# A spectral filter and a gated feed-forward layer on one core: every step in a new order, and some sums and low parts on GpSimd

## The chip, the core and the metric

The kernel runs on one core of a Trainium2 chip. The number that counts is the device time of one execution in microseconds, the median of several runs. The kernel before takes 406.75 us (runs of 407.12, 405.2 and 406.75). TensorE (PE) does the matmuls, VectorE (DVE), ScalarE (ACT) and GpSimd (POOL) the elementwise work. The hardware queue of transfers is issued by SyncE (SP); POOL issues a queue of its own.

## The reference

```python
xn = (x - mean(x)) / sqrt(var(x) + 1e-5)          # x: 2048 x 512
X = rfft2(xn) * (w_r + 1j * w_i)                   # over both axes; 2048 x 257 bins
s = irfft2(X)                                      # 2048 x 512
gate = xn @ W_gate; up = xn @ W_up                 # 512 -> 1376 each
h = where(gate > 0, gate, 0) * up
g = silu(h @ W_down)                               # 1376 -> 512
out = x + s * g
```

## The kernel before

Both halves are matmuls. A number is held as a high and a low f16 part, and each product is made in three passes (high by high, high by low, low by high).

**Feed-forward half.** The 2048 rows are four blocks of 512, the 1376 hidden columns eleven groups of 128 (the last, number 10, has 96). `gu` is a PSUM tile of a gate or an up product (12 matmuls of 512 columns); there are three buffers of it. ACT makes `r` = relu(gate), DVE `h32` = gate times up, ACT its high part `h16`, DVE the low part, and `dn` is the product with W_down, 512 columns by 128 rows of output at a time, one PSUM buffer. ACT turns it into the gate `g`.

For some pairs of hidden groups in the last block, `fast_products` (L1049) makes the four products of a pair from fewer matmuls with sums of rows (`xS`) and of weights (`wT`, made by `weight_sums`, L788, from the weights in `rp`): three PSUM tiles `sa`, `sb`, `sc` take products of 256 columns in turn, ACT copies `sb`<-`sa`, `sk`<-`sc`, DVE adds `sc`, `se`<-`sb`+`sk`, ACT relus to `sr` and `sq`, and DVE multiplies. PE cannot make the next product into `sb` or `sc` before these are through. In the rows of the order below, `se3_4` is the `se` of block 3, pair 4, and `sv4_4640` the `sv` of chunk 4 (the last number is the instance); the trace leaves the numbers out.

**Spectral half.** Two-dimensional transforms as matmuls with constant matrices: `s` (rows), `y`, `xx` (columns), then the filter on DVE and POOL (`tt` products, their sums `pf`, rounded to `p`), and back by `z`, `v` and a second `s`. There are eight chunks. `fold` (L651) prepares the sums and differences of a chunk's input. `last_stage` (L1293) of chunk c takes the second `s` from PSUM with ACT (`zz`), makes sums and differences (`ae`, `ye`, `sv`), and `finish` (L1342) multiplies `sv` by `g`. The second `s` needs a PSUM buffer of the same ring as `gu`.

**Output.** For chunks 0, 1, 3 and 4 (`ADDS`, L45) the copy of x goes to `out` first and `sv` is then added by a DMA on POOL's queue, `out<-sv`, two per chunk. For the others DVE adds x in the tile `xt`, which SP stores. `sv`, `ye`, `eo`, `x` and more share a ring of ten buffers, `k4` (`ROOM`, L56): whoever takes a buffer waits until the last reader of its former holder is done, and where this is a DMA, until it has landed. `columns` (L172) parts the last 128 rows of output into 256, 128 and 128 columns (`dn_3`, `dn_3b`, `dn_3bb`), so that the last gate, multiply, add and store are smaller.

**Order.** All work is stated as steps of one engine with a cost, what they read and write, and a due time. `Plan.run` (L244) places them one by one: on each engine, of the steps that can begin soonest, that with the earliest due time. Due times and the lead with which some steps may begin come from two tables of numbers (`DUES`, `WAITS`). The order that results is the order of the instructions on each engine, which then waits in line: an instruction that waits holds up all behind it. Every instruction goes through the one helper at L189, so all rows of the trace name that line (in the changed kernel, which has one line more, L190).

Lists of engine names say where some work is done: `FOLDS`, `SUM2` (the sums `tt` and `pf`), `DIFF2` (`ae`), `TSUMS` (sums of weights of a pair), `SECONDS` and `HLOWS` (the second multiply, `se`, and the low parts in `fast_products`). In `fast_products` the multiply is `lambda: eng.tensor_mul(T[E], T[E], T[r2])` (L1095): it looks up `eng` when it is run, and by then the loop behind it has set `eng` anew, to the engine of the pair's second low part. Its cost and its place in the plan are those of `SECONDS`.

Of the kernel before, what the change touches and what calls it, by code (L numbers as in the profile page):

```python
# [54 lines left out]
SUM2, DIFF2 = ['POOL', 'POOL', 'DVE', 'POOL', 'DVE', 'DVE', 'POOL', 'DVE', 'POOL', 'DVE', 'DVE', 'POOL', 'POOL', 'DVE', 'DVE', 'POOL'], ['DVE', 'POOL', 'POOL', 'POOL', 'POOL', 'DVE', 'DVE', 'DVE', 'POOL', 'DVE', 'POOL', 'DVE', 'POOL', 'DVE', 'DVE', 'POOL']  # L55
ROOM = {"k4": 10, "k2": 8, "kg": 4, "cm": 3, "h16": 11, "xg": 3, "F": 2, "gu": 3, "dn": 1, "q": 4, "q4": 2, "mv": 4, "m": 4, "p": 4, "am": 1, "mid": 3}  # L56
CALM, SAFE, SAFE_LAG, RATE, TURNKB = 40, 1.0, 1.0, 320, 1300
SUMS, TSUMS, FMARGIN = ['DVE', 'DVE', 'DVE', 'DVE'], ['DVE', 'DVE', 'DVE', 'DVE', 'DVE'], 0.4
SECONDS, HLOWS = ['DVE', 'DVE', 'DVE', 'DVE', 'DVE', 'DVE', 'DVE', 'DVE', 'DVE', 'DVE', 'DVE', 'DVE', 'DVE', 'DVE', 'DVE', 'DVE', 'DVE', 'DVE', 'DVE', 'DVE'], ['DVE', 'DVE', 'DVE', 'DVE', 'DVE', 'DVE', 'DVE', 'DVE', 'DVE', 'DVE', 'DVE', 'DVE', 'DVE', 'DVE', 'DVE', 'DVE', 'DVE', 'DVE', 'DVE', 'DVE', 'DVE', 'DVE', 'DVE', 'DVE', 'DVE', 'DVE', 'DVE', 'DVE', 'DVE', 'DVE', 'DVE', 'DVE', 'DVE', 'DVE', 'DVE', 'DVE', 'DVE', 'DVE', 'DVE', 'DVE']
# [311 lines left out]
def kernel(ctx: ExitStack, tc: tile.TileContext, x, wg, wu, wd, wl, ew, sp, c_r, c_d, c_m, c_x, c_s, out):  # L371
    nc = tc.nc
    PS = bass.MemoryType.PSUM
    PE, DVE, ACT, POOL, SP = (InOrder(tc, e) for e in (nc.tensor, nc.vector, nc.scalar, nc.gpsimd, nc.sync))
# [47 lines left out]
    step = T.step  # L422
# [1139 lines left out]
```

## Time and profile before

| | |
|---|---|
| median of three runs | 406.75 us (405.2 to 407.12) |
| profiled execution | 405.83 us |
| its span, first to last instruction | 404.1 us |
| busy PE / DVE / ACT / POOL | 395.1 / 327.0 / 234.7 / 30.3 us |
| granted clock of PE | 1.00 |

The profiled execution's 405.83 us is 1.7 us more than the span that the trace covers, and 0.9 us less than the median of the runs. A busy PE is not a PE at its peak, since matmuls overlap; but an idle PE is plain. Idle time of the other engines costs only where somebody waits for it, and a wait in a queue is charged to the instruction that waits, though those behind it pay too.

### The profile page before, as it was taken

The page shows a single profiled execution, that of the slowest core. Times are in us where ns is not written, and L with a number is a line of the kernel's source. Part 1 is how long each engine was busy: PE and PEld are TensorE (multiplying, and loading weights), DVE is VectorE, ACT ScalarE, POOL GpSimd, SP SyncE. Part 2 cuts the span into 40 slices and gives each one's busy share as a digit, 9 for nine tenths or more (in the row PEclk, how much of TensorE's full clock was granted, in tenths as well). Part 3 has the DMA queues.
Part 4 walks back from the last instruction along what each step waited for, and adds up shares of the span by engine and source line. Part 5 has one row for each costly group of instructions (what it writes and reads, how often), then busy time and mean ns, then how long its engine had stood idle before and what let it go on. Part 6 is the DMA issues. An engine that isn't in the chain of part 4 may idle for free.

```text
span 404.1 us, 8177 instructions
## 1 busy us (share of the span) xinstructions
PE 395.1 (98%) x3152; PEld 225.6 (56%) x3152; DVE 327.0 (81%) x733; ACT 234.7 (58%) x458; POOL 30.3 (8%) x48
## 2 busy tenths in 40 slices
PE   8999999999999999999999999999999999989995
PEld 7864444444444454565564545646557767766455
DVE  4899999998889899457749699889973838779985
ACT  6899986788668785141345454746335636634321
POOL 0000000000000000003101001020110003303300
PEclk9999999999999999999999999999999999999999
DMA  7955004824996668831053445368391499649654
GB/s 262 407 223 174 0 2 110 182 57 138 300 309 183 170 220 289 280 82 52 26 170 84 141 128 173 86 200 212 79 233 55 131 217 253 121 120 195 166 191 149
DMA packets 52791, 66.37 MB, mean 164 GB/s; under 512 B 20432, under 2 KB 30256, under 8 KB 52752
## 3 DMA queue, kind: packets, MB, share of 16 engines
q1 hardware_dynamic: 51600, 63.76, 53.4%
q0 software_dynamic: 1152, 2.10, 3.5%
q8 instruction: 24, 0.39, 0.4%
q14 instruction: 15, 0.12, 0.1%
HBM read 42.76 MB, written 20.99 MB: 158 GB/s over the span
## 4 chain that ended last, share of the span: by engine, by line
PE 89%; DMA 4%; ACT 4%; DVE 1%; issue 0%; SPq 0%; POOL 0%; DVEq 0%; ACTq 0%
PE gu L189 42%; PE dn L189 27%; PE sb L189 3%; PE s L189 3%; PE z L189 3%; PE xx L189 3%; ACT wgu L189 2%; PE sa L189 2%; PE sc L189 2%; DMA out<-sv 2%; PE y L189 2%; PE v L189 2%; DMA raw<-in_wu 2%; DVE sv L189 1%; DMA x<-in_x 1%; PE dn_3bb L189 0%
## 5 line engine op out<-in xcount | busy, mean ns | idle before, releaser
L189 PE MATMUL gu<-xT,wgu 128*128 128x512 f16 (+1 forms) x768 | 167.2, 372 | 0.9 <-ACT r L189 0.6
L189 PEld LDWEIGHTS <-wgu 128*128 128x128 f16 x960 | 92.7, 98 | 87.4 <-issue 3.7
L189 PE MATMUL dn<-wds,h 128*128 128x512 f16 (+2 forms) x528 | 116.9, 372 | 0.0
L189 PEld LDWEIGHTS <-h 128*128 128x128 f16 (+1 forms) x594 | 54.4, 98 | 56.5 <-issue 2.2
L189 DVE TENSOR_TENSOR h<-gu,r 128x512 f32<-128x512 f32 (+3 forms) x44 | 27.6, 627 | 10.0 <-PE gu L189 8.9
L189 ACT ACTIVATE r<-gu 128x512 f32<-128x512 f32 (+2 forms) x36 | 20.9, 579 | 25.1 <-PE gu L189 25.0
L189 ACT ACTIVATE h<-h 128x512 f16<-128x512 f32 (+1 forms) x36 | 22.4, 625 | 21.0 <-DVE h L189 20.7
L189 DVE TENSOR_TENSOR h<-h,h 128x512 f16<-128x512 f32 (+1 forms) x36 | 25.1, 700 | 2.5 <-ACT h L189 2.1
L189 POOL TENSOR_TENSOR tt<-tt,tt 128x256 f32<-128x256 f32 x8 | 7.7, 963 | 246.2 <-DVE tt L189 226.9
L189 DVE SCALAR_TENSOR_TENSOR tt<-xsp,cw,wt 128x512 f32<-128x512 f32 x32 | 22.9, 761 | 0.2
L189 ACT ACTIVATE g<-dn,cdi 128x512 f32<-128x512 f32 (+1 forms) x16 | 10.6, 670 | 19.4 <-PE dn L189 15.6
L189 ACT ACTIVATE p<-pf 128x1024 f16<-128x1024 f32 x8 | 8.5, 1057 | 16.5 <-DVE pf L189 15.2
L189 PE MATMUL gu<-xT,wgt 128*64 128x256 f16 (+1 forms) x144 | 17.0, 309 | 0.0
L189 DVE TENSOR_TENSOR z<-z,z 128x1024 f16<-128x1024 f32 x8 | 9.8, 1223 | 8.4 <-ACT z L189 8.3
L189 PEld LDWEIGHTS <-wT 128*128 128x128 f16 x144 | 13.8, 98 | 4.5 <-issue 1.9
L189 DVE SCALAR_TENSOR_TENSOR wgu<-raw,p,wgu 128x512 f16<-128x512 f32 x20 | 14.2, 743 | 0.0
L189 DVE TENSOR_TENSOR xsp<-xx,xo 128x256 f32<-128x256 f32 (+1 forms) x16 | 5.0, 352 | 10.9 <-ACT xsp L189 9.1
L189 PEld LDWEIGHTS <-wgt 128*64 128x64 f16 (+1 forms) x144 | 9.6, 106 | 7.1 <-issue 1.5
L189 ACT ACTIVATE wgu<-raw 128x512 f16<-128x512 f32 x20 | 12.4, 621 | 1.4 <-DMA raw<-in_wu 0.7
L189 PE MATMUL sb<-xS,wT 128*128 128x256 f16 x96 | 11.8, 273 | 1.3 <-DVE sv L189 1.3
L189 POOL TENSOR_TENSOR ae<-zz 128x128 f32<-128x128 f32 (+1 forms) x16 | 8.8, 599 | 53.6 <-ACT zz L189 41.8
L189 DVE TENSOR_TENSOR t<-s,t 128x128 f16<-128x128 f32 (+1 forms) x16 | 10.5, 685 | 2.3 <-ACT t L189 2.3
(197 smaller groups left out, 604.8 us busy)
## 6 DMA issues: line engine op xcount, KB each, us to landing
A_d<-t SPq DMA_DIRECT2D x16, 256.0 KB, 3.5
rw<-in_wl SPq DMA_DIRECT2D x8, 512.0 KB, 5.0
wt<-in_wl SPq DMA_DIRECT2D x8, 512.0 KB, 4.6
at<-A_d SPq DMA_DIRECT2D x8, 512.0 KB, 4.9
C_d<-t SPq DMA_DIRECT2D x16, 256.0 KB, 3.5
ct<-C_d SPq DMA_DIRECT2D x16, 256.0 KB, 7.5
x<-in_x SPq DMA_DIRECT2D x7, 512.0 KB, 4.1
G_d<-g SPq DMA_DIRECT2D x12, 256.0 KB, 2.3
```

The source lines that it names most:

```text
L189: return lambda *args, **kw: self.tc.keep_in_program_order(f(*args, **kw))
```

## The change

Nothing that is computed changes: PE has the same 3152 matmuls. What changes are the numbers of the planner, and the engines named in the lists:

```diff
-FOLDS, FOLD_LEAD, MARGIN = ['DVE', 'DVE', 'DVE', 'DVE', 'DVE', 'DVE', 'DVE', 'DVE'], 78.705, 1.95
+FOLDS, FOLD_LEAD, MARGIN = ['DVE', 'DVE', 'DVE', 'DVE', 'DVE', 'POOL', 'DVE', 'DVE'], 78.705, 1.95
-NORMS = ['DVE', 'DVE', 'DVE', 'DVE', 'DVE', 'ACT', 'ACT', 'DVE', 'DVE', 'DVE', 'ACT', 'DVE', 'DVE', 'ACT', 'DVE', 'DVE']
+NORMS = ['DVE', 'DVE', 'DVE', 'DVE', 'ACT', 'DVE', 'ACT', 'ACT', 'DVE', 'ACT', 'DVE', 'DVE', 'DVE', 'DVE', 'DVE', 'DVE']
-SUM2, DIFF2 = ['POOL', 'POOL', 'DVE', 'POOL', 'DVE', 'DVE', 'POOL', 'DVE', 'POOL', 'DVE', 'DVE', 'POOL', 'POOL', 'DVE', 'DVE', 'POOL'], ['DVE', 'POOL', 'POOL', 'POOL', 'POOL', 'DVE', 'DVE', 'DVE', 'POOL', 'DVE', 'POOL', 'DVE', 'POOL', 'DVE', 'DVE', 'POOL']
+SUM2, DIFF2 = ['POOL', 'POOL', 'POOL', 'POOL', 'POOL', 'POOL', 'POOL', 'POOL', 'POOL', 'POOL', 'POOL', 'POOL', 'DVE', 'DVE', 'POOL', 'DVE'], ['POOL', 'POOL', 'DVE', 'DVE', 'DVE', 'DVE', 'POOL', 'DVE', 'DVE', 'DVE', 'DVE', 'DVE', 'DVE', 'DVE', 'DVE', 'DVE']
-SUMS, TSUMS, FMARGIN = ['DVE', 'DVE', 'DVE', 'DVE'], ['DVE', 'DVE', 'DVE', 'DVE', 'DVE'], 0.4
+SUMS, TSUMS, FMARGIN = ['DVE', 'DVE', 'DVE', 'DVE'], ['POOL', 'DVE', 'POOL', 'DVE', 'POOL'], 0.4
-SECONDS, HLOWS = ['DVE', 'DVE', 'DVE', 'DVE', 'DVE', 'DVE', 'DVE', 'DVE', 'DVE', 'DVE', 'DVE', 'DVE', 'DVE', 'DVE', 'DVE', 'DVE', 'DVE', 'DVE', 'DVE', 'DVE'], ['DVE', 'DVE', 'DVE', 'DVE', 'DVE', 'DVE', 'DVE', 'DVE', 'DVE', 'DVE', 'DVE', 'DVE', 'DVE', 'DVE', 'DVE', 'DVE', 'DVE', 'DVE', 'DVE', 'DVE', 'DVE', 'DVE', 'DVE', 'DVE', 'DVE', 'DVE', 'DVE', 'DVE', 'DVE', 'DVE', 'DVE', 'DVE', 'DVE', 'DVE', 'DVE', 'DVE', 'DVE', 'DVE', 'DVE', 'DVE']
+SECONDS, HLOWS = ['DVE', 'DVE', 'DVE', 'DVE', 'DVE', 'DVE', 'DVE', 'DVE', 'DVE', 'DVE', 'DVE', 'DVE', 'DVE', 'DVE', 'DVE', 'DVE', 'DVE', 'DVE', 'DVE', 'DVE'], ['DVE', 'DVE', 'DVE', 'DVE', 'DVE', 'DVE', 'DVE', 'DVE', 'DVE', 'DVE', 'DVE', 'DVE', 'DVE', 'DVE', 'DVE', 'DVE', 'DVE', 'DVE', 'DVE', 'DVE', 'DVE', 'DVE', 'DVE', 'DVE', 'DVE', 'DVE', 'DVE', 'DVE', 'DVE', 'DVE', 'DVE', 'POOL', 'DVE', 'DVE', 'DVE', 'POOL', 'POOL', 'POOL', 'DVE', 'DVE']
+DEVIATE = (2.68, 2.54, 2.54)
 DUES = (
-    9.45, 123.13, 114.11, 124.55, 1e+09, 1e+09, 1e+09, 1e+09, 1e+09, 1e+09, 1e+09, 1e+09, 1e+09, 1e+09, 1e+09, 1e+09, 1e+09, 1e+09, 1e+09, 1e+09,
...
+    22.97, 129.83, 142.84, 147.2, 1e+09, 1e+09, 1e+09, 1e+09, 1e+09, 1e+09, 1e+09, 1e+09, 1e+09, 1e+09, 1e+09, 1e+09, 1e+09, 1e+09, 1e+09, 1e+09,
...
 WAITS = (
-    7.16, 8.31, 9.25, 95.27, 18.97, 77.25, 61.2, 65.23, 46.59, 33.23, 54.73, 90.53, 33.33, 3.56, 7.82, 116.65, 68.38, 18.19, 7.93, 12.13, 24.01,
...
+    12.95, 9.5, 13.45, 77.89, 13.68, 27.76, 43.2, 22.88, 66.81, 18.05, 88.78, 26.95, 66.35, 2.7, 3, 127.06, 47.09, 50.7, 25.11, 41.31, 30.03, 18.56,
...
-        step("DVE", 2.4 + .14 * sum("ACT" in NORMS[2 * c:2 * c + 2] for c in cs), run, reads=[(f"mv{c}", i) for c in cs for i in range(2 + (STATS[c] == "ACT"))], writes=[(name, 2)], port=True)
+        step("DVE", DEVIATE[cs[0] // 2 - 1], run, reads=[(f"mv{c}", i) for c in cs for i in range(2 + (STATS[c] == "ACT"))], writes=[(name, 2)], port=True)
```

All numbers of `DUES` and `WAITS` are new; a line of each is shown. POOL has 13 entries of `SUM2` where it had 8, and 3 of `DIFF2` where it had 8 (an entry is two instructions). `DEVIATE` is a cost that the planner reckons with and changes no instruction. The entries 31, 35, 36 and 37 of `HLOWS` are low parts in the last block: pair 0's and pair 2's second, and both of pair 3. By the late look-up of `eng` the second multiplies `se` of these three pairs go to POOL too, while the plan has them on DVE.

The first place is SP's queue at the start: the loads of x (`x`), of the gate and up weights (`raw_0`, `raw_1`) and of the constant matrix `cR`. Before:

```order
L189 DMA x_141<-in_x 128x512 x2
L189 DMA raw_1_148<-in_wu 128x512
L189 DMA raw_0_153<-in_wg 128x512
L189 DMA cR<-in_c_r 128x512
L189 DMA x_169<-in_x 128x1024
L189 DMA raw_0_173<-in_wg 128x512
L189 DMA raw_1_186<-in_wu 128x512
```

and now:

```order
L190 DMA x_141<-in_x 128x512 x2
L190 DMA raw_0_148<-in_wg 128x512
L190 DMA raw_1_153<-in_wu 128x512
L190 DMA x_168<-in_x 128x1024
L190 DMA raw_0_172<-in_wg 128x512
L190 DMA raw_1_185<-in_wu 128x512
L190 DMA raw_0_194<-in_wg 128x512
```

with `cR` further behind in the same queue:

```order
L190 DMA raw_1_238<-in_wu 128x1024
L190 DMA raw_1_251<-in_wu 128x896
L190 DMA x_254<-in_x 128x1024
L190 DMA wds<-in_wd 128x3x512
L190 DMA cR<-in_c_r 128x512
```

The load of `cR`, 128 KB, has gone from ahead of the second chunk of x to behind the first load of W_down.

The second place is ACT's queue in the last stages, where a new `sv` takes the buffer in which chunk 1's `sv` was (the wait for two DMASW semaphores is that for its two `out<-sv`). Before, chunk 4's `sv` (`sv4_4640`) takes it:

```order
L189 ACTIVATE h16_3_3_1_4637<-se3_3_4611 128x512 [waits DVE_49]
L189 ACTIVATE sv4_4640<-ye4_4460 128x4 [waits DMASW1_49,DMASW0_49]
L189 ACTIVATE r3_3_4657<-gu3_3_0_4617 128x512 [waits DMAHW3_49,PE_49]
L189 ACTIVATE sv0_4665<-ye0_4559 128x4 [waits DVE_49,Activation_49,Pool_49]
L189 ACTIVATE sv3_4681<-ye3_4593 128x4 [waits DVE_49,Activation_49]
L189 ACTIVATE h16_3_3_0_4688<-sr3_3_4566 128x512 [waits DVE_49]
L189 ACTIVATE sb3_4_4704<-sa3_4_4667 128x512 [waits PE_49]
```

and now chunk 3's (`sv3_4700`), with other work behind it:

```order
L190 ACTIVATE sv4_4697<-ye4_4446 128x4 [waits DVE_49,Activation_49]
L190 ACTIVATE sv3_4700<-ye3_4614 128x4 [waits DMASW1_49,DMASW0_49]
L190 ACTIVATE ye2_4621<-ae2_4568 128x2 [waits DVE_49]
L190 ACTIVATE h16_3_3_0_4710<-sr3_3_4387 128x512
L190 ACTIVATE zz7_4726<-s2_7_4640,cwi_111 128x1024 [waits DVE_49,PE_49,Activation_49]
L190 ACTIVATE zz6_4746<-s2_6_4669,cwi_111 128x1024 [waits DMAHW6_49,DMAHW3_49,PE_49]
L190 ACTIVATE ye7_4751<-zz7_4726 128x2 [waits DMAHW7_49,DMAHW0_49,Activation_49]
L190 ACTIVATE sr3_4_4767<-sa3_4_4599 128x512 [waits PE_49,Pool_49]
```

The wait stands as before, but the relu `r3_3` and the copy of `sa3_4` to `sb3_4` are no longer behind it; the high part of `sr3_3`, the `zz` of chunks 7 and 6 and the relu `sr3_4`, which also waits for POOL, are. DVE has the same wait at its own part of `sv3_4700`.

The third place is POOL's queue in those stages, before:

```order
L189 DMA out_0<-sv1_4414 128x512 x2
L189 TENSOR_TENSOR ae0_4554<-zz0_4534 128x2x63
L189 DMA out_0<-sv4_4640 128x512
L189 DMA out_0<-sv0_4665 128x512 x2
L189 DMA out_0<-sv3_4681 128x512 x2
L189 TENSOR_TENSOR ae5_4914<-zz5_4896 128x2x64
L189 DMA out_0<-sv4_4640 128x512
```

and now:

```order
L190 DMA out_0<-sv1_4415 128x512
L190 TENSOR_TENSOR ae3_4547<-zz3_4524 128x2x64 x2
L190 DMA out_0<-sv1_4415 128x512
L190 TENSOR_TENSOR h16_3_3_0_4710<-sr3_3_4387,h16_3_3_0_4710 128x512
L190 DMA out_0<-sv0_4577 128x512 x2
L190 DMA out_0<-sv4_4697 128x512
L190 DMA out_0<-sv3_4700 128x512
L190 TENSOR_TENSOR se3_3_4543<-se3_3_4543,sq3_3_4572 128x512
L190 DMA out_0<-sv3_4700 128x512
L190 TENSOR_TENSOR h16_3_3_1_4832<-se3_3_4543,h16_3_3_1_4832 128x512
L190 DMA out_0<-sv4_4697 128x512
```

The multiply `se3_3` and two low parts of pair 3 now stand among the additions to `out`.

The last place is the end of SP's queue, before:

```order
L189 DMA out<-xt_1_5103 128x512
L189 DMA out<-xt_1_5121 128x512
L189 DMA out<-xt_1_5074 128x128 x2
L189 DMA out<-xt_0_5129 128x512
L189 DMA out<-xt_1_5074 128x256
```

and now:

```order
L190 DMA out<-xt_0_5066 128x512
L190 DMA out<-xt_0_5060 128x512
L190 DMA out<-xt_0_5090 128x512
L190 DMA out<-xt_1_5068 128x256
L190 DMA out<-xt_1_5068 128x128 x2
```

The part of 256 columns of the last 128 rows of output has gone from last to third last; PE's last matmuls are now of `dn_3b`, 128 columns, in place of `dn_3`, 256.

More of the change, by code (lines that the diff above doesn't have):

```diff
@@ L64 @@
 XDUE, SDUE = [-18.3, 7.83, 88.22, 100.36, 188.84, 115.24, 195.7, 156.37], [-84.52, 3.8, 95.3, 188.33]
+DEVIATE = (2.68, 2.54, 2.54)
 DUES = (
-    9.45, 123.13, 114.11, 124.55, 1e+09, 1e+09, 1e+09, 1e+09, 1e+09, 1e+09, 1e+09, 1e+09, 1e+09, 1e+09, 1e+09, 1e+09, 1e+09, 1e+09, 1e+09, 1e+09,
+    22.97, 129.83, 142.84, 147.2, 1e+09, 1e+09, 1e+09, 1e+09, 1e+09, 1e+09, 1e+09, 1e+09, 1e+09, 1e+09, 1e+09, 1e+09, 1e+09, 1e+09, 1e+09, 1e+09,
     1e+09, 1e+09, 1e+09, 1e+09, 1e+09, 1e+09, 1e+09, 1e+09, 1e+09, 1e+09, 1e+09, 1e+09, 1e+09, 1e+09, 1e+09, 1e+09, 1e+09, 1e+09, 1e+09, 1e+09, 1e+09,
-    1e+09, 1e+09, 1e+09, 1e+09, 1e+09, -211.71, -49.3, -65, -49.5, -49.61, -49.7, -48.72, -47.53, -40.01, -55.32, -41.85, -48.21, -52.55, -46.66,
[83 rows of a table removed]
+    1e+09, 1e+09, 1e+09, 1e+09, 1e+09, -128.45, -85.36, -83.53, -85.74, -105.37, -88.74, -74.4, -87.39, -83.45, -82.92, -84.78, -81.82, -80.12,
[83 rows of a table added]
 )
 WAITS = (
[12 rows of a table removed]
[12 rows of a table added]
 )
```

188 rows, old and new, of tables (DUES, WAITS) are left out of this document.

## The prediction

> **What bounds the kernel now.** First the page: who is busy, where POOL works, and who ends the chain of waits.
>
> ```profile
> PE 395.1 (98%) x3152; PEld 225.6 (56%) x3152; DVE 327.0 (81%) x733; ACT 234.7 (58%) x458; POOL 30.3 (8%) x48
> ...
> POOL 0000000000000000003101001020110003303300
> ...
> PE 89%; DMA 4%; ACT 4%; DVE 1%; issue 0%; SPq 0%; POOL 0%; DVEq 0%; ACTq 0%
> ```
>
> PE is busy in 98% of the span and has 89% of the chain. DVE, the second, has 327.0 us and 1% of the chain: taking work from DVE is worth only what PE waits for DVE. So the question is where PE is idle. The view of busy time by stretch of 10 us has PE at 10.00 everywhere but in these seven rows:
>
> ```profile
> 0.00:10.00 10.00, 8.80 (x62) 7.13 (x63) 4.63 (x19) 6.49 (x16) 1.00 (x8) 1.00 0.77 260
> 10.00:20.00 10.00, 9.30 (x77) 8.20 (x76) 8.41 (x27) 8.96 (x25) 0.00 (x0) 1.00 1.03 408
> 20.00:30.00 10.00, 9.44 (x71) 6.65 (x69) 9.14 (x32) 9.61 (x28) 0.00 (x0) 1.00 0.62 233
> 90.00:100.00 10.00, 9.66 (x65) 4.38 (x64) 8.85 (x28) 8.74 (x18) 0.00 (x0) 1.00 0.43 130
> 350.00:360.00 10.00, 8.13 (x62) 5.82 (x60) 7.39 (x20) 4.07 (x10) 0.00 (x0) 1.00 0.58 148
> 390.00:400.00 10.00, 9.77 (x95) 7.21 (x93) 8.38 (x18) 1.79 (x5) 0.00 (x0) 1.00 0.52 177
> 400.00:404.10 4.10, 0.00 (x0) 0.00 (x0) 0.85 (x2) 0.28 (x1) 0.00 (x0) 1.00 0.29 104
> ```
>
> (The columns behind the stretch are its length and the busy time of PE, PEld, DVE, ACT and POOL.) Idle PE in them: 1.20, 0.70, 0.56, 0.34, 1.87, 0.23 and 4.10 us, together 9.0 of the span's 404.1. The first of 1.20 and most of the last 4.10 are the entry of the first data and the way of the last result to memory. What an order can win is the middle: at most 0.70 + 0.56 + 0.34 + 1.87 + 0.23 = 3.7 us, and some tenths at both ends.
>
> The largest piece is in the last stages, by the timeline there (the square brackets hold the idle time ahead of the row and what ended it; behind a row of several instructions they speak of the first):
>
> ```profile
> 347.59 0.68 DVE L189 TENSOR_TENSOR sv<-sv,g_2l 128x512 f32<-128x512 f32 x1
> ...
> 348.58 0.87 POOL L189 DMA_DIRECT2D out<-sv  x1 [0.30 <-DVE ae L189]
> ...
> 353.26 0.63 ACT L189 ACTIVATE h<-se 128x512 f16<-128x512 f32 x1 [1.18 <-DVE se L189]
> ...
> 356.50 0.21 ACT L189 ACTIVATE sv<-ye 128x4 f32<-128x4 f32 x1 [2.61 <-DMA out<-sv]
> 356.51 1.29 DVE L189 TENSOR_TENSOR sv<-ye 128x510 f32<-128x510 f32 x2 [2.61 <-DMA out<-sv]
> 356.62 0.58 ACT L189 ACTIVATE r<-gu 128x512 f32<-128x512 f32 x1
> ...
> 357.25 1.47 PE L189 MATMUL sc<-xS,wgu 128*128 128x256 f16 x12 [0.59 <-ACT r L189]
> ...
> 358.12 0.68 DVE L189 TENSOR_TENSOR sr<-sb,sr 128x512 f32<-128x512 f32 x1
> ...
> 360.00 1.25 PE L189 MATMUL sb<-xS,wT 128*128 128x256 f16 x10 [1.29 <-DVE sv L189]
> ```
>
> The second `out<-sv` of chunk 1 leaves POOL at 348.58. ACT is through with its `h` at 353.89 and then stands 2.61 us, until 356.50; so does DVE. Both wait to write a new `sv` into the buffer that this DMA reads, and the chain says when it lands:
>
> ```profile
> 348.58 7.84 DMA out<-sv
> ```
>
> 348.58 + 7.84 = 356.42. Behind the waiting instructions stand ACT's `r` (it frees a PSUM buffer for PE's `sc`, which starts 0.59 us late) and DVE's `sr` (it frees `sb`, 1.29 us late). 0.59 + 1.29 = 1.88 us is all that PE loses there; the other 0.7 us of the 2.61 is hidden under matmuls that were ready.
>
> **The change part by part.** *Work moved from DVE to POOL.* By the listed order POOL gets twelve sums of weights, three `se` multiplies and four low parts, all 128x512, the ten sums of one fold, and ten `tt`/`pf` more and ten `ae` less. What such work costs:
>
> ```profile
> 359.92 0.41 DVE L189 TENSOR_TENSOR ye<-ae,zz 128x254 f32<-128x254 f32 x1
> ...
> 360.59 0.68 DVE L189 TENSOR_TENSOR h<-h,h 128x512 f16<-128x512 f32 x1
> ```
> ```profile
> 183.89 1.10 POOL L189 TENSOR_TENSOR tt<-tt,tt 128x256 f32<-128x256 f32 x1 [179.89 <-DVE tt L189]
> ...
> 185.63 0.72 POOL L189 TENSOR_TENSOR tt<-tt,tt 128x256 f32<-128x256 f32 x1
> ```
>
> DVE takes 0.68 us for 512 columns and 0.41 for some 256 (so about 0.28 for 128). It is relieved of 19 x 0.68 = 12.9 us, and some 4 of the fold, while `tt` and `ae` about cancel: 17 of 327.0. On POOL 256 columns take 0.72 us with DVE quiet and 1.10 beside it; 512 columns are not in the trace, so from 1.44 to 2.2 us by twice these rows, and 1.44 is nearer, since the planner keeps such steps apart. That is 19 x 1.44 = 27 us, with the fold and `tt` some 36 in all, on an engine that was busy 30.3. On the path this is worth nothing by itself: PE did not wait for DVE except for the 1.29 above. If the cover went (DVE falling behind PE), each us late would cost one; that is the third rival.
>
> *The last stages.* The stall is not removed: chunk 1's buffer still has a follower, now chunk 3's `sv`. What changes is who stands behind. I count PE's work from the end of the `s` of chunk 1, by 1.31 us for 12 matmuls of 256 columns, 2.59 for 12 of 512, 0.72 for an `s`. DVE reaches `se3_3` when PE's second product into `sb3_3` ends, at 11.0; then 0.6 for it, 0.33 for one `ye`, 4 x 0.33 for four, 1.28 for two pieces of `sv`, 0.6 for the multiply (durations as above, less the 0.08 by which one overlaps the next): the store can leave at 15.3. From issue to landing:
>
> ```profile
> out<-sv POOLq DMA_DIRECT2D x8, 256.0 KB, 6.6
> ```
>
> 6.6 at the median, 7.84 in the row above: it lands at 21.9 to 23.1. ACT, at rest in the queue by then, goes on with `sv`, `ye` and `h16` (0.2, 0.2, 0.63) and the `zz` of chunk 7, of which two take this:
>
> ```profile
> 345.51 2.12 ACT L189 ACTIVATE zz<-s,cwi 128x1024 f32<-128x1024 f32 x2 [0.77 <-PE s L189]
> ```
>
> So 2.1 us behind the landing, at 24.0 to 25.2, PE gets the PSUM buffer for `gu` of group 10, which by its own work it could start at 23.7. PE idles 0.3 to 1.5 us, where I take 1.0 (DVE also has waits of its own), in place of 1.88: **-0.9**. Bounds: nothing left at the short landing (-1.9), and as long a stall again on top where both the landing is the longer and POOL's low part of `h16_3_3_0` holds `sr3_4` (+1.0). That low part, 1.44 to 2.2 us behind its high part, lets `sr3_4` end at 25.0 to 27.0, and the next `gu` needs it at 23.7 + 1.0 + 2.6 = 27.3: it is hidden, with 0.3 to spare at worst.
>
> *The start.* `cR` no longer stands ahead of the second x:
>
> ```profile
> 2.60 0.43 SPq L189 DMA_DIRECT2D cR<-in_c_r  x1
> ```
>
> 128 KB at the 260 to 408 GB/s of the first two stretches is 0.50 to 0.32 us that everything behind it lands earlier. On the chain of waits the load behind it leads to PE's gap of 0.69:
>
> ```profile
> 4.75 6.09 DMA raw<-in_wu
> ```
> ```profile
> 12.28 0.38 PE L189 MATMUL small<-m,ones 128*128 128x2 f32 x2 [0.69 <-ACT wgu L189]
> ...
> 25.67 1.03 PE L189 MATMUL gu<-xT,wgu 128*128 128x256 f16 x8 [0.56 <-ACT r L189]
> ```
>
> I take **-0.3**: not more, since ACT is 9 of 10 us busy from 10 to 30 and its own work sets the second gap (0 to -0.9).
>
> *The end.* PE's last matmuls, of 256 columns, end where ACT's last `g` can begin, at 399.8; then (ahead of it a `g` of 128 columns)
>
> ```profile
> 396.20 0.37 ACT L189 ACTIVATE g<-dn_3b,cdi 128x128 f32<-128x128 f32 x1
> ...
> 399.81 0.47 ACT L189 ACTIVATE g<-dn,cdi 128x256 f32<-128x256 f32 x1 [3.24 <-PE dn L189]
> 400.31 0.43 DVE L189 TENSOR_TENSOR sv<-sv,g 128x256 f32<-128x256 f32 x1 [1.02 <-ACT g L189]
> 400.77 0.42 DVE L189 TENSOR_TENSOR xt<-xt,sv 128x256 f32<-128x256 f32 x1
> ```
>
> 0.47 + 0.43 + 0.42, and the store until 404.1. With 128 columns it is 0.37 + 0.28 + 0.28: 0.39 less, and a store of half the bytes: **-0.45** (-0.7 to -0.2).
>
> *Switches of PE's tile.* A `gu` behind an `s` (64 rows of the array) takes 0.11 us more:
>
> ```profile
> 110.97 2.59 PE gu L189 x12
> 113.56 1.44 PE s L189 x48
> 115.00 2.70 PE gu L189 x12
> ```
>
> PE changes tile 53 times before and 51 now: **-0.2** (both ways certain to a tenth).
>
> *The gap at 98 us.*
>
> ```profile
> 98.50 2.75 PE gu L189 x12
> ```
>
> It is the time that PE runs out of work while ACT makes a `g`. In the new order 1.94 us of matmuls (nine of 512 columns) stand between, where 1.3 (six) stood: **-0.2** (0 to -0.34).
>
> *New small waits.* All else has been re-sorted too, and some margins are smaller: counted by the same durations, ACT reaches the scale of the sixth group of weights some 3 us ahead of PE where it was 7. I put **+0.3** (0 to +2), as one more gap of the size of those at 98 and 25 us.
>
> Sum: -0.9 - 0.3 - 0.45 - 0.2 - 0.2 + 0.3 = -1.75 us, a span of 402.35. The profiled execution of before took 405.83, 1.7 more than its span, and the median of the runs is 0.9 above it; so 404.1 for a profile, and **405.0** for the median, 0.43% less.
>
> **The rivals.** *All gaps close.* If the store lands early enough (the 6.6 us, or less), the last-stage stall goes whole, and with it both gaps of the start in part: -1.9 - 0.9 - 0.45 - 0.2 - 0.3 = -3.7, **403.0**. For it speaks that every wait named here has 1 us or less to close; against it that the same buffer conflict is still in the queue, and that before its store took 7.84.
>
> *The stall only moves.* The wait at `gu` of group 10 is as long as the 1.88 was, and the start is bound by ACT: with the end and the switches -0.65, and +0.4 of new gaps, **406.5**. For it: PE is the bound, DVE's relief buys nothing, and ACT's queue in the new order has more behind the wait. Against it: the count above.
>
> *POOL holds up DVE.* The trace has a place where both want their operands at once:
>
> ```profile
> 195.80 1.89 POOL L189 TENSOR_TENSOR pf<-tt,tt 128x256 f32<-128x256 f32 x2 [8.75 <-PE dn L189]
> 196.26 0.84 DVE L189 TENSOR_TENSOR tt<-tt,tt 128x256 f32<-128x256 f32 x1
> ```
>
> The `tt` of 256 columns took 0.84 us on DVE, beside 0.41 in the row above, and POOL's two `pf` 1.89 instead of 1.44. If every new POOL instruction held DVE so, the last stages would pay: four `ae` of chunk 0 on POOL ahead of DVE's `sv` of chunk 1 (4 x 0.42 = 1.7 later store), a landing of 7.84 (+1.2 on the shorter), and `h16_3_3_0` and `se3_3` at 2.2 each in POOL's queue between five DMA issues, so that DVE's `se3_4`, for which PE's last product of pair 4 waits, loses its margin of about 1 us and 1.5 more. Stalls of 1.0 + 1.7 + 1.2 + 1.5 = 5.4 in place of 1.88 are +3.5, less 0.95 of the rest: **409.3**. It decides from the point where POOL costs DVE over 2 us in the 20 us ahead of `se3_4`. For it: the row; against it: only some pairs meet, and before there were more `ae` on POOL at this place. The Trainium skill ("SBUF — State Buffer", section "Who interferes with whom") goes further than the row: a DVE instruction with two SBUF inputs and a GpSimd one that reads SBUF block each other for the whole instruction. By that, the 36 us more of POOL work could all come back on DVE, which the 0.42 lost of 1.89 in this row doesn't bear out in full.
>
> **How the numbers follow.** The forecast has 0.45, all gaps close 0.22, the stall only moves 0.16, POOL holds up DVE 0.17. Under 0.5%, or 2.0 us, a measurement of this kernel can't tell a change from none: faster means below 404.7, slower above 408.8. The forecast's own range is 403.5 to 406.3, a little below the middle of which 404.7 lies: 0.18 faster, 0.27 same. The first rival is faster; the second same, but for 0.01; the third slower in 0.15 and same in 0.02. Faster 0.40, same 0.44, slower 0.16. The range is 402.5 (every idle us in the middle won) to 408.9 (short of the third rival).
>
> **What would show it.** In the profile after: 1.0 us idle PE at a `gu` some 24 us behind the `s` of chunk 1, ended by ACT's `zz`, with ACT's wait ended by `out<-sv`; the first 30 us with some 2.2 idle instead of 2.46; last matmuls of 128 columns, and the span ending about 3.9 us behind them; the 10-us stretches between 30 and 340 at 10.00. POOL 65 us or more, DVE about 310. Wrong it would be with a PE gap ended by POOL, or by DVE beside a long POOL row; with new gaps between 40 and 50 (weights that come late); or with no gap at all near 350.

## The result, and the profile after

The changed kernel takes 409.27 us (median of six runs, 407.86 to 410.55), the kernel before, run beside it, 406.44 (six runs, 405.2 to 407.12). The ratio is 1.0072, with a 95% interval of 1.0043 to 1.01: slower by 0.7%, where 405.0 was forecast, and above the top of the range, 408.9. The profiled execution of the changed kernel took 407.86 us, its span 405.8; before, 405.83 and 404.1.

From the page of after: the busy times, POOL by slices, and the shares of the chain of waits.

```profile
PE 395.1 (97%) x3152; PEld 226.1 (56%) x3152; DVE 319.8 (79%) x702; ACT 233.2 (57%) x458; POOL 67.0 (17%) x78
...
POOL 0000000000540014003343031200040622334000
...
PE 77%; DVE 10%; ACT 5%; DMA 4%; issue 2%; SPq 1%; DVEq 0%; ACTq 0%
```

PE is busy for the same 395.1 us, so every microsecond lost is idle PE. DVE has lost 7.2 us of work and now has 10% of the chain where it had 1%: the chain now runs through DVE's work ahead of the store that is shown below. In the view by stretches of 10 us these rows of after have PE below 10.00 (columns as in the prediction: length, then busy PE, PEld, DVE, ACT, POOL, and PE's granted clock):

```profile
0.00:10.00 10.00, 8.80 (x61) 7.12 (x62) 5.12 (x20) 6.29 (x15) 0.99 (x8) 1.00 0.80 263
20.00:30.00 10.00, 9.39 (x70) 6.64 (x69) 9.36 (x33) 9.86 (x29) 0.00 (x0) 1.00 0.63 237
90.00:100.00 10.00, 9.81 (x46) 4.36 (x45) 8.36 (x30) 9.97 (x21) 0.00 (x0) 1.00 0.19 66
140.00:150.00 10.00, 8.82 (x82) 4.41 (x82) 5.86 (x15) 5.24 (x11) 0.00 (x0) 1.00 0.60 196
150.00:160.00 10.00, 7.79 (x74) 4.29 (x73) 6.62 (x13) 7.39 (x14) 5.61 (x4) 1.00 0.72 196
360.00:370.00 10.00, 8.70 (x82) 4.81 (x81) 9.97 (x15) 6.44 (x18) 8.09 (x8) 1.00 0.75 119
370.00:380.00 10.00, 9.77 (x64) 6.11 (x63) 9.88 (x22) 3.02 (x7) 0.00 (x0) 1.00 0.61 159
400.00:405.80 5.80, 2.06 (x37) 1.89 (x34) 2.02 (x6) 0.79 (x3) 0.00 (x0) 0.88 0.14 45
```

Against the rows of before, idle PE has changed like this: the first 30 us 2.46 to 1.81 (-0.65), the gap at 98 us 0.34 to 0.19 (-0.15), the last stages 1.87 to 1.30 + 0.23 (-0.34), the end behind 390 us 0.23 + 4.10 to 3.74 (-0.59). All the places that the prediction spoke of got better, by 1.73 us together. Then there are two rows that have no counterpart: 1.18 and 2.21 us between 140 and 160 us, where before had 10.00 twice. 3.39 - 1.73 is 1.66, and the span grew by 1.7.

What happens there, in the timeline of after (`t` is the first transform's result, rounded, `X_d` the copy of a chunk's normalized rows in memory):

```profile
140.56 0.34 SPq L190 DMA_DIRECT2D X_d<-x  x1
...
145.63 1.89 ACT L190 ACTIVATE t<-s 128x128 f16<-128x128 f32 x3 [2.78 <-DMA X_d<-x]
146.75 2.29 DVE L190 TENSOR_TENSOR t<-s,t 128x128 f16<-128x128 f32 x3 [3.14 <-ACT t L190]
...
148.10 2.76 PE L190 MATMUL gu<-xT,wgt 128*128 128x512 f16 x12 [1.18 <-DVE t L190]
...
150.79 0.85 PE L190 MATMUL s<-xs,cR 64*64 64x257 f16 x24
...
152.19 1.04 ACT L190 ACTIVATE junk<-rw 128x1024 f16<-128x1024 f32 x1
...
153.23 0.57 ACT L190 ACTIVATE r<-gu 96x512 f32<-96x512 f32 x1
...
153.86 1.50 PE L190 MATMUL gu<-xT,wgt 128*64 128x256 f16 x24 [2.21 <-ACT r L190]
```

SP issues the store `X_d<-x` of chunk 7 at 140.56. ACT, free since 142.85, has a new `t` to write (`t1_5`) into the buffer that the store reads, and stands 2.78 us until 145.63. The chain has the store's landing:

```profile
140.56 4.99 DMA X_d<-x
```

140.56 + 4.99 = 145.55. The PSUM buffer of that `s` comes free late, when DVE's part of `t` is through too, and PE's next `gu`, which takes it (only the `gu` of group 10 shares a ring of PSUM buffers with the `s`), begins 1.18 us late; ACT then has its queue of `r`, `junk`, `h`, `rp`, a second `h` and `junk` still before it and reaches the `r` of the gate of 96 columns at 153.23, for which PE stands another 2.21. So one wait costs PE twice. It is the same kind as the one in the last stages: an ACT instruction whose new tile gets a buffer of the ring `k4` that a transfer, not yet landed, still reads.

The profile is the shortest of the six executions. Its granted clock was 0.998; three of the six had 0.994 to 0.995 (410.55, 409.93 and 409.6 us, on average 410.03) and the others 0.998 and more (407.86, 408.94, 408.5, on average 408.43). That is a second loss of 1.6 us, in half of the executions, which the profile of after doesn't show; an experiment's does.

### The profile page after: what moved, and what is told of

Same layout as the page of the kernel before. It is cut to its first block, busy times and chain, and to the rows that moved or that the text cites. A ratio compares the mean times of both kernels' runs of the same rounds, so it can differ in the third digit from the quotient of the medians.

```text
span 405.8 us, 8203 instructions
## 1 busy us (share of the span) xinstructions
PE 395.1 (97%) x3152; PEld 226.1 (56%) x3152; DVE 319.8 (79%) x702; ACT 233.2 (57%) x458; POOL 67.0 (17%) x78
## 4 chain that ended last, share of the span: by engine, by line
PE 77%; DVE 10%; ACT 5%; DMA 4%; issue 2%; SPq 1%; DVEq 0%; ACTq 0%
PE gu L190 32%; PE dn L190 24%; PE sb L190 4%; PE z L190 3%; PE xx L190 3%; PE sc L190 2%; PE sa L190 2%; DVE h L190 2%; ACT xf L190 2%; PE y L190 2%; PE s L190 2%; PE small L190 2%; PE v L190 2%; DVE xs L190 1%; DMA X_d<-x 1%
## 5 line engine op out<-in xcount | busy, mean ns | idle before, releaser
L190 POOL TENSOR_TENSOR tt<-tt,tt 128x256 f32<-128x256 f32 x14 | 12.0, 864 | 75.7 <-DVE tt L190 75.7
L190 POOL TENSOR_TENSOR rp<-rp 128x512 f32<-128x512 f32 x12 | 15.7, 1312 | 52.0 <-ACT rp L190 51.3
L190 POOL TENSOR_TENSOR pf<-tt,tt 128x256 f32<-128x256 f32 x12 | 9.7, 821 | 36.5 <-DVE tt L190 36.5
L190 ACT ACTIVATE z<-z 128x1024 f16<-128x1024 f32 x8 | 8.2, 1024 | 11.3 <-PE z L190 11.3
```

The costliest lines, as they stand in the source:

```text
L190: return lambda *args, **kw: self.tc.keep_in_program_order(f(*args, **kw))
```

## The experiments

Each group of four kernels ran on one chip with the kernel before among them: 405.9 us for the first four (chip 1), 405.9 for the second four (chip 9), 405.73 for the third (chip 11). Ratios are against those. All edits but those marked "before" are to the changed kernel.

### One buffer of its own for `t1_5`

Theory A: the wait for this buffer is the whole of the loss. The room for one more buffer comes from the weight sums of pair 1, which are allotted and never used.

```diff
-    wT = [wpool.tile(..., name=f"wT{n}") for n in range(len(PAIRS))]
+    wT = [wpool.tile(..., name=f"wT{n}") if n != 1 else None for n in range(len(PAIRS))]
...
-tile(shape, dtype, name=name, tag=tag, bufs=T.room[tag])
+tile(shape, dtype, name=name, **(dict(tag="own", bufs=1) if name in ('t1_5',) else dict(tag=tag, bufs=T.room[tag])))
```

> The changed kernel in the same order, but chunk 5's first-stage result (t1_5) gets a buffer of its own in place of the next of the k4 ring (room for it comes from the weight sums of pair 1, which nothing uses). Theory A, the buffer turn: t1_5 waits there for the store of chunk 7's x to land, and both gaps of PE at 148 and 154 (1.18 + 2.21 = 3.4 us) come from it: both go, 409.3 -> about 405.9. Theory B, ACT's own queue: the relu behind the second gap is late because ACT first makes other work in the new order; then only the first gap goes and 1.5 to 2.2 stays: about 407.5 to 408. Theory C, POOL holding up DVE: no change within 0.5 us.

405.54 us (ten runs), ratio 0.9996 (0.9984 to 1.0009). The ACT and PE rows of its timeline:

```profile
143.22 1.88 ACT L190 ACTIVATE t<-s 128x128 f16<-128x128 f32 x3
...
147.37 2.75 PE L190 MATMUL gu<-xT,wgt 128*128 128x512 f16 x12
...
151.43 1.50 PE L190 MATMUL gu<-xT,wgt 128*64 128x256 f16 x24 [0.53 <-ACT r L190]
```

ACT goes on without a wait (no bracket), 3.39 us of idle PE become 0.53, and all ten executions have a clock of 0.998 or more. By the ratios the buffer is worth 0.76%, 3.1 us (0.96% against the second set of runs of the changed kernel, below): 2.86 of the gaps, and what the clock costs on the median; in this profile a gap of 0.69 at 12 us, absent from that of after, takes some of it back. What makes the kernel slower is this one wait for a buffer. The other wait for this ring that costs PE stays: in the last stages every tile still gets the buffer of the same former holder, and the stall at 360 us is there again, with 1.39 us. The run also shows that the rest of the change, all of POOL's new work with it, comes out even with the kernel before.

### The same in the last stages, of both kernels

For the stall at 360 us `sv3` gets a buffer of its own in the changed kernel, and `sv4` in the kernel before: the same edit with the other name.

```diff
-... if name in ('t1_5',) else ...
+... if name in ('sv3',) else ...
```

> The changed kernel in the same order, chunk 3's sv in a buffer of its own, so that nothing waits for the landing of chunk 1's addition to out at 360. Theory A: the gap of 1.30 us at the gu of group 10 goes, and nothing else: 409.3 -> 408.0. Theory C: DVE behind POOL is late there anyway and PE keeps 0.7 us or more of it: 408.7 or above.

> The kernel before in its own order, chunk 4's sv in a buffer of its own: the wait for chunk 1's addition to out at 356 goes. Theory A: the two gaps of 0.59 + 1.29 = 1.88 us go: 406.4 -> 404.6. If other work behind is late too, less than 1 us.

The changed kernel: 408.15 us (four runs), ratio 1.0059 (1.0037 to 1.0081). Before with its buffer: 404.08 (four runs), 0.9953 (0.9935 to 0.997). The groups of PE at the place in question, of the changed kernel with `sv3` apart:

```profile
362.30 1.89 PE L190 MATMUL gu<-xT,wgt 128*128 128x512 f16 x8 [0.31 <-ACT zz L190]
```

and of before with `sv4` apart, its two stretches:

```profile
350.00:360.00 10.00, 10.00 (x83) 7.83 (x81) 9.79 (x24) 5.10 (x17) 0.34 (x1) 1.00 0.65 156
360.00:370.00 10.00, 10.00 (x91) 6.83 (x92) 9.86 (x19) 3.19 (x6) 3.50 (x4) 1.00 0.97 210
```

1.30 falls to 0.31 in the one, 1.87 to nothing in the other, where 1.8 us come off the median (with a new gap of 0.42 at 119 us). In the changed kernel the median can't show it: 1.0059 lies inside the interval of the kernel without the edit. Nor is the wait itself gone, though that was expected. The next taker of a buffer gets that of chunk 1's `sv`: in the changed kernel `zz` of chunk 7,

```profile
361.13 2.12 ACT L190 ACTIVATE zz<-s,cwi 128x1024 f32<-128x1024 f32 x2 [2.01 <-DMA out<-sv]
```

and in the kernel before `sv0`, for which ACT waits 1.62 us, DVE 0.21 and PE not at all. So the stall was read rightly in both orders: its price is set by what stands behind the wait. In the kernel before, one more buffer takes more of it than the new order does.

### POOL's work back on DVE

The same order, with only the engine changed that the moved sums, second multiplies and low parts are issued to; the planner's costs stay.

```diff
-        e, eng, cost = (("DVE", DVE, dve), ("POOL", POOL, pool))[SECONDS[5 * c + n] == "POOL"]
+        e, eng, cost = (("DVE", DVE, dve), ("POOL", DVE, pool))[SECONDS[5 * c + n] == "POOL"]
...
-            e, eng, cost = (("DVE", DVE, dve), ("POOL", POOL, pool))[HLOWS[10 * c + 2 * n + m] == "POOL"]
+            e, eng, cost = (("DVE", DVE, dve), ("POOL", DVE, pool))[HLOWS[10 * c + 2 * n + m] == "POOL"]
```

and alike for the fold, the weight sums and those `SUM2` that were on DVE before. Once on the changed kernel, and once with the ring of eleven buffers (below), where ACT doesn't wait at 145 us:

> The changed kernel in the same order, with the work that the change moved to POOL done by DVE again at the same places of the order (sums of weights, the fold of chunk 5, the second multiplies and low parts of the last block, the five added tt/pf pairs). Theory C, POOL costs the time (DVE rows beside POOL are up to 1.5 us longer): faster by 1.5 us or more, 407.8 or less. Theory A: the gaps at 148 are ahead of nearly all of it and stay: the same within 1 us, or slower where DVE, now with some 17 us more, falls behind PE (up to +2).

> The changed kernel with a k4 ring of eleven and the moved work done by DVE again. With the waits for buffers in, moving it back gave 407.95 where the changed kernel had 409.3 to 409.7. Theory C2, POOL's share costs time on PE's path by itself: again 1.0 us or more faster than 403.3. Theory A2, it only shortened or lengthened the same waits (and the share of runs with a low clock): the same within 0.5 us of 403.3, or slower where DVE falls behind.

On the changed kernel 407.95 us (eight runs), ratio 1.0047 (1.002 to 1.0073); the two gaps are still there, 0.95 and 2.21 us, and the store leaves at 140.14, 0.4 us earlier: POOL's part in making it late is no more than that. With the ring of eleven 403.59 (six runs), ratio 0.9937 (0.9919 to 0.9954), beside 403.31 with POOL's work on POOL (0.9939, 0.9921 to 0.9958): no difference. Their busy times, of this kernel

```profile
PE 394.3 (98%) x3152; PEld 225.9 (56%) x3152; DVE 327.6 (82%) x746; ACT 234.2 (58%) x458; POOL 23.1 (6%) x34
```

and of the ring of eleven alone:

```profile
PE 395.8 (98%) x3152; PEld 226.6 (56%) x3152; DVE 318.3 (79%) x702; ACT 233.7 (58%) x458; POOL 67.2 (17%) x78
```

44 us of POOL and 9 us of DVE more or less make nothing here, on a path that PE sets. The 1.3 us by which the first of the two kernels is below 409.27 is more than the one theory allows and less than the other asks for; it is within intervals that overlap, and lies in part in its clock (low in two of eight executions, not three of six) and shorter gaps; how much is POOL's isn't settled by it.

### Is it the clock: more work in the gaps

The changed kernel again, for its spread, and two kernels that give PE something to do where it stands. The one makes the first transform of chunk 7 four times over (64 rows of the array), the other the gate product of group 10 of block 1 twice; both do this work in vain, on top of the whole computation.

```diff
-            for a, b, m in RANGES:
+            for a, b, m in RANGES * (4 if c == 7 else 1):
```
```diff
-            for k in range(4):
+            for k in [0, 1, 2, 3] * (2 if (c, f, i) == (1, TAIL, 0) else 1):
+                n %= 12
```

> The changed kernel once more, unaltered, to stand beside the others on the same chip. If PE's clock is what spreads its runs (0.994 or 0.995 in the three slower ones, 0.998 or 0.999 in the three faster, 1.6 us apart), the runs fall into two groups again, some 408.4 and 410.0.

> The changed kernel with the first-stage product of chunk 7 made four times instead of once (the same numbers into the same place), so that PE works through the gap of 2.2 us at 152 in place of standing still; the wait itself stays, and nothing behind it can start earlier. Theory D, the gap makes PE's clock fall behind it in some executions: the clock stays at 1.00 in all runs, the median falls by 0.5 to 1.2 us against the changed kernel and the spread to 1.5 us or less. If the clock has nothing to do with the gap: the same median (0 to +0.3 us) and the same spread of 2.7 us.

> The changed kernel with the gate product of group 10 of block 1 made twice (the same numbers into the same place), so that PE has 2.6 us more of matmuls that use all 128 rows just ahead of the gap of 2.2 us. The filling with products of 64 rows left the spread and the low clocks as they were. Theory D2, such narrow products don't count as work for the clock, wide ones do: all runs at 0.998 or above, and a median 0.5 us or more below the changed kernel's (409.3 to 409.7). Theory D3, the first gap of 1 to 2 us ahead (the wait for DVE) is enough to make the clock fall: runs of 0.994 to 0.996 remain, median 409.5 to 410.

The changed kernel again: 409.69 us (six runs, ratio 1.0092, 1.0068 to 1.0116), three executions with a clock of 0.994 to 0.996. With the transform: 409.72 (1.0101), three of six at 0.996. With the gate product: 409.94 (1.0103), one of six at 0.995. Over the six of the changed kernel again and the six of after, the executions at 0.996 or less take 410.29 us on average, those at 0.998 or more 408.62: 1.67 us. Where it is lost, the profile of the kernel with `sv3` apart shows, one of its executions at 0.996 (columns as above, the granted clock behind POOL):

```profile
153.00:154.00 1.00, 0.54 (x10) 0.53 (x11) 0.00 (x0) 1.00 (x2) 0.92 (x2) 1.00 0.73 180
154.00:155.00 1.00, 1.00 (x17) 0.98 (x14) 0.59 (x1) 1.00 (x4) 1.00 (x1) 0.67 0.77 307
155.00:156.00 1.00, 1.00 (x7) 0.28 (x3) 1.00 (x3) 0.41 (x1) 0.92 (x2) 0.50 0.26 90
156.00:157.00 1.00, 1.00 (x3) 0.30 (x2) 0.97 (x3) 0.90 (x1) 0.44 (x1) 0.50 0.07 16
157.00:158.00 1.00, 1.00 (x4) 0.40 (x3) 0.17 (x1) 0.25 (x2) 0.00 (x0) 0.62 0.99 213
158.00:159.00 1.00, 1.00 (x6) 0.48 (x5) 0.00 (x0) 0.00 (x0) 0.00 (x0) 1.00 0.96 268
```

From 154.3 to some 157.6 PE has half its clock, right behind the second gap. (The profile with POOL's work back on DVE, an execution at 0.995, has it too: 0.50 from 155 to 157 us.) The same twelve matmuls there, in that kernel and then in after:

```profile
155.37 3.92 PE L190 MATMUL gu<-xT,wgu 128*128 128x512 f16 x12
```
```profile
155.29 2.76 PE L190 MATMUL gu<-xT,wgu 128*128 128x512 f16 x12
```

1.16 us more, and 0.47 more in the group ahead of them (1.97 for 1.50): 1.63 together, the 1.6 by which executions differ. The two fillings don't cure it in the time: the first keeps the low clock in three of six though its second gap is down to 0.23 in the profile (the first was 1.89), and in the second the low clock is seen once in six, but its first gap, behind a store that left at 142.00 in place of 140.56, was 2.81 in the profile,

```profile
150.16 5.35 PE L190 MATMUL gu<-xT,wgt 128*128 128x512 f16 x24 [2.81 <-DVE t L190]
```

so that its median is no lower. So the expectation that work in the gaps brings back clock and time fell, or at least wasn't met: on what the clock needs the two are inconclusive. What stands are the counts: of 24 executions with both gaps (after, `sv3` apart, POOL's work on DVE, after again) 10 are at 0.996 or less, of 56 of the kernels without the pair not one is below 0.997.

### Both buffers, and one more for all

If both waits are of the ring, two buffers or an eleventh for the whole ring should take both. The ring of eleven also for the kernel before:

```diff
-tile(shape, dtype, name=name, tag=tag, bufs=T.room[tag])
+tile(shape, dtype, name=name, tag=tag, bufs=T.room[tag] + (tag == "k4"))
```

> The changed kernel in the same order with both waits for a buffer gone (t1_5 and sv3 share one buffer of their own, 200 us apart). Theory A: the gains of the two add up, against the kernel before -0.2 (the first alone) and -1.1 of the second: some 404.6 where before is at 405.9. If the second wait only hides another one, 405.3 or more.

> The changed kernel in the same order (the planner still counts ten buffers), but the k4 ring has eleven, in the room that the unused weight sums left: every taker of a buffer waits for a holder one further back. Theory A: both waits go, and any smaller ones of this ring too: 404.6 or a little less, as with buffers of their own. If only these two tiles are special (their own DMA late), one or both come back with another tile in the turn: above 405.5.

> The kernel before in its own order with a k4 ring of eleven. Theory A: the wait for chunk 1's addition to out goes, as with a buffer of its own (404.1, 1.8 less than before), unless another tile comes into that turn. Against the changed kernel with eleven (403.3) it shows what the new order is worth without the waits for buffers: the sum of the prediction's other terms, some 0.8 to 1.1 us in its favour.

| kernel | us | ratio to before |
|---|---|---|
| changed, `t1_5` and `sv3` apart (12 runs) | 404.61 | 0.9971 (0.9961 to 0.9981) |
| changed, ring of eleven (6) | 403.31 | 0.9939 (0.9921 to 0.9958) |
| before, ring of eleven (6) | 403.67 | 0.9945 (0.993 to 0.9961) |

Two buffers apart leave 1.12 us at 151 us (ended by ACT's `r`) and 0.82 at 359 (ended by `zz`, which waits 2.52 us for `out<-sv` there) and still bring the changed kernel below the one before; beside `t1_5` apart alone the second buffer is worth 0.25%, 1.0 us. The eleventh buffer turns the change from 2.8 us slower into 2.6 faster than the kernel before, and gives the kernel before 2.1 us by itself. With it the two orders are 0.06% apart, which these runs can't tell from nothing, where 0.8 to 1.1 us in favour of the new order were expected.

The eleventh buffer does not do it as expected, by moving every taker to an older holder. By the addresses in the built program `t1_5` still has the buffer that the store of chunk 7 reads, and `zz` of chunk 7 has that of chunk 1's `sv`. What has changed at the first place is the store:

```profile
139.64 0.34 SPq L190 DMA_DIRECT2D X_d<-x  x1
...
142.46 1.90 ACT L190 ACTIVATE t<-s 128x128 f16<-128x128 f32 x3 [0.25 <-PE s L190]
```

It lands in 2.7 us, where it took 5.0 (and in 2.6 with POOL's work on DVE), just before ACT comes to `t1_5`. The loads `rw` and `rp` ahead of it in SP's queue left at 138.82 and 139.20 in after, 1.7 and 1.4 us before the store; here they leave at 135.98 and 136.40, 3.7 and 3.2 before it, since `rw` gets a buffer that is free earlier. That the store is short because these transfers are out of its way is likely, but no run has that alone. At the second place the ring still bites:

```profile
358.02 2.12 ACT L190 ACTIVATE zz<-s,cwi 128x1024 f32<-128x1024 f32 x2 [1.73 <-DMA out<-sv]
...
359.18 2.75 PE L190 MATMUL gu<-xT,wgt 128*128 128x512 f16 x12 [1.08 <-ACT zz L190]
```

`zz` of chunk 7 waits for an `out<-sv`, and PE stands 1.08 us for it, about as much as the new order was expected to be ahead. One more buffer changes who waits and when loads leave, not only how long a wait is.

### The load of `cR` later, alone

The kernel before, with this load moved behind the first load of W_down in SP's queue, as in the changed one:

```diff
+        at = [i for i, (t, s) in enumerate(order) if s.engine == "SP"]
+        load = next(i for i in at if "cR" in order[i][1].names)
+        moved = order.pop(load)
+        order.insert(next(i for i, (t, s) in enumerate(order) if s.engine == "SP" and any("wd" in str(n) for n in s.names)) + 1, moved)
```

> The kernel before with only the load of the matrix cR moved in SP's queue from ahead of the second x to behind the first load of W_down, as the changed kernel has it. The prediction's term: 0.3 us faster (0 to 0.9). If the gap at 12 us comes and goes with the loads' luck whatever the order: no change (within 0.2).

405.94 us (twelve runs), ratio 1.0002 (0.9992 to 1.0013): nothing. The gap of 0.69 at 12 us is absent from this profile, but it comes and goes between kernels whose start is the same: 0.69 in the profile of the changed order with `t1_5` apart, 0.44 with both buffers apart, 0.29 with `sv3` apart, none in that of after; and none in two more profiles of the order before (`sv4` apart, ring of eleven), whose `cR` is where it was. One profile can't carry a term of 0.3 us at the start.

## Why the prediction was wrong, by its own steps

**What bounds the kernel** held. PE is the bound, and the span of the profiles went with idle PE to within 0.1 us.

**Work moved to POOL.** Its price on POOL was about right, that on DVE too low, and neither mattered. The twelve sums of 512 columns cost less than the 1.44 us that I took:

```profile
L190 POOL TENSOR_TENSOR rp<-rp 128x512 f32<-128x512 f32 x12 | 15.7, 1312 | 52.0 <-ACT rp L190 51.3
```

1.31 us each, and POOL's 67.0 us are the 65 and more that were expected. But DVE, expected at 310, is at 319.8: it gets only 7 of the 17 us back. Rows side by side in the last stages of after show where such time goes:

```profile
366.15 1.90 DVE L190 TENSOR_TENSOR ye<-zz,ae 128x254 f32<-128x254 f32 x1
366.18 1.58 POOL L190 TENSOR_TENSOR se<-se,sq 128x512 f32<-128x512 f32 x1
...
368.51 1.27 POOL L190 TENSOR_TENSOR h<-se,h 128x512 f16<-128x512 f32 x1
368.57 1.77 DVE L190 TENSOR_TENSOR h<-h,h 128x512 f16<-128x512 f32 x1
```

DVE's `ye` took 1.90 us in place of 0.41, its `h` 1.77 in place of 0.68: both end when POOL's instruction has ended and most of their own time has passed (366.18 + 1.58 = 367.76, and 0.29 to the end of `ye` at 368.05; 368.51 + 1.27 = 369.78, and 0.56 to 370.34). Here DVE loses nearly the whole of POOL's instruction (1.49 of 1.58 and 1.09 of 1.27 us), and not the 0.42 of 1.89 from which I doubted the rule. This agrees with the Trainium skill ("SBUF — State Buffer", section "Who interferes with whom"), by which such a pair block each other. The two rows are 2.6 us of the ten; the others weren't added up. In the row that I held against it both sides had lost, `tt` 0.84 - 0.41 = 0.43 us and the two `pf` 1.89 - 1.44 = 0.45, which fits their taking turns as well as it fits sharing.

**The last stages, -0.9**, was right in place and cause and too large by half a microsecond. Idle PE there fell by 0.34, not 0.9: it stood 1.30 us at `gu` of group 10, where 1.0 was forecast, and 0.23 at an `sb`. The rows name what was named:

```profile
360.18 0.21 ACT L190 ACTIVATE sv<-ye 128x4 f32<-128x4 f32 x1 [3.00 <-DMA out<-sv]
...
360.90 2.10 ACT L190 ACTIVATE zz<-s,cwi 128x1024 f32<-128x1024 f32 x2
362.05 2.75 PE L190 MATMUL gu<-xT,wgt 128*128 128x512 f16 x12 [1.30 <-ACT zz L190]
```

**The end, -0.45**, was right. The last rows of the timeline before the store:

```profile
401.06 1.00 PE L190 MATMUL dn_3b<-wds,h 128*128 128x128 f16 x15
...
402.10 0.37 ACT L190 ACTIVATE g<-dn_3b,cdi 128x128 f32<-128x128 f32 x1 [0.47 <-PE dn_3b L190]
402.50 0.29 DVE L190 TENSOR_TENSOR sv<-sv,g 128x128 f32<-128x128 f32 x1 [0.22 <-ACT g L190]
402.83 0.29 DVE L190 TENSOR_TENSOR xt<-xt,sv 128x128 f32<-128x128 f32 x1
```

From PE's last matmul to the end are 3.74 us (402.06 to 405.8) where there were 4.33 (399.77 to 404.1): -0.59.

**The gap at 98 us, -0.2**: -0.15, right. **Switches of PE's tile, -0.2**: not to be seen, with PE busy 395.1 us both times. **The start, -0.3**: wrong in its cause. The first 30 us were 0.65 shorter in this one profile, but the moved load is worth nothing (405.94 beside 405.73), so this is the gap that comes and goes.

**New small waits, +0.3 (0 to +2)**, is the step that failed. They came to 3.39 us of idle PE, and to some 0.8 more on the median by the clock (1.6 in half of the executions). What I had done was to follow the buffer wait to where the trace of before had it, at 350 us, and to check the rest of the order by how far ACT and PE are ahead of one another. Yet the row was in the new order before any run, in ACT's and SP's queues:

```order
L190 ACTIVATE t1_5_1852<-s1_5_1803 128x2x64 [waits DMAHW3_49,PE_49]
L190 DMA X_d7_79<-x16_7_1705 128x2048 [waits DMAHW3_49,DVE_49]
```

A compute instruction that reads only PSUM, and writes a tile of `k4`, waits for a DMA: that can only be a buffer's last reader. Before, `t1_5` also waited for transfers, but others, and PE had 10.00 in both stretches. To price the new wait I needed the time from issue to landing of such a store, 4.1 to 4.8 us in the profile of before, and how far ACT's work reaches behind the issue, 2.3 us by the rows of after (140.56 to 142.85), for which the order would have had to be counted: 1.8 to 2.5 us of wait, where 2.78 came, in a queue on which PE's next `gu` depends. The planner can't see it either, by its own code: it takes for a new tile the buffer of the ring that is free soonest,

```python
t = max(t, sorted(room[tag])[k - 1] + .15)   # L296
```

and counts a transfer as done when it has landed. The pool from which the tiles come does otherwise: by the addresses in the built program, 146 of the 160 tiles that take over a buffer get the one whose former holder's last use stands first in the listed order, and there a transfer stands where it is issued. So `t1_5` got the buffer of the store, issued ahead of the last use of every other holder. The claim that the stretches between 30 and 340 us would be at 10.00 fell with it.

The sum makes this plain: the five named terms were -2.05, and the profiles have -1.73 for them. With 3.39 in place of 0.3 for the rest the span would have been forecast at 404.1 - 2.05 + 3.39 = 405.4, and it was 405.8. Of the 4.3 us by which the median of 409.27 missed 405.0, 3.45 are this span (405.8 for 402.35); the other 0.8 are that the median lies 3.5 us above it, where 2.6 were taken from the kernel before, which is about the share of the clock.

**The rivals.** "All gaps close" and "the stall only moves" spoke of the right places and missed the new one. "POOL holds up DVE" had the right time, 409.3, by coincidence, and the wrong cause: the blocking is there, fuller than I thought, but both gaps stay when POOL's work goes back to DVE, and the loss goes when `t1_5` has a buffer of its own. By the time alone this rival would have looked proven.

## What to carry to other kernels

When an order changes, go through all waits of compute instructions for a DMA in the new order, not only those that hurt in the old one: each such wait on an instruction whose inputs are not loaded is for a buffer that a transfer still reads, and costs from the issue to the landing of that transfer (here 5 us), less what stands between. A planner that counts free buffers must choose among them as the pool does. Here a spare buffer was worth more than the new order (2.1 us by itself, beside 0.06% for the order with it, which is not told from nothing), and an unused tile had the memory for it; but read the new profile too, since the spare one also changes who gets which buffer. Judge what an off-path engine's work costs by taking it away where nothing else stalls.

## What the runs showed of the hardware that was not expected

**PE's clock fell to a half behind gaps of 1 and 2 us.** With 0.9 to 1.2 us of idle PE, some 3.5 us of matmuls and 2.21 us of idle PE in the profiles, 10 of 24 executions had a mean clock of 0.996 or less; the two of them that were profiled had 0.50 for some 3 us behind the second gap, and such executions are 1.6 us longer. No gap there reached the 3.4 us for which the Trainium skill gives the loss of the clock as a rule ("TensorE: Matmul & The Clock Gate", section "HAM oscillation — how this bites in real kernels"); that the clock falls to a half and comes back after about that long agrees with the table in its Part 1. Why some of the executions and not all, the runs don't show; nor do the two fillings tell whether it is the sum of the gaps or how weakly PE is used between them, and the first of them had the low clock with hardly a second gap.

**One store took 2.6 to 5.6 us to land.** From the issue of chunk 7's `X_d<-x` to ACT going on there are 5.0 to 5.7 us in the six profiles with this wait, and in the two of the changed order with a ring of eleven the store lands in 2.6 and 2.7. PE's first gap went from 0.88 to 2.81 in those six, a third of it by this time and the rest mostly by when the store was issued (140.14 to 142.00). A wait that looks small in one profile isn't bounded by it.
